# Keys before the query weights, one batch's cache rows per load, and transposed keys in the ring of load slots

## The chip, the core and the metric

The kernel runs on one core of a Trainium2 chip. The core has a matrix engine (PE, or TensorE), two engines for elementwise work (DVE, or VectorE, and ACT, or ScalarE), a general engine (POOL), and a queue engine (SP) that here issues the large loads; 16 DMA engines carry them out. On-chip memory (SBUF) has 128 partitions; a matrix product lands in a second, small memory (PSUM) of eight banks. The metric is the device time of one launch, in microseconds (us). A time of a profiled launch is its span, from the first to the last instruction, and a little around it.

## The reference

One decoding step for four sequences of one token: a pre-normed attention with a cache, and a gated feed-forward layer.

```python
W = 2048                                        # last 2048 cache rows
q = layernorm(x) @ wq                           # x 4 x 1024, wq 1024 x 4096: 32 heads of 128
k = k_cache[:, :, Sk - W:, :]                   # 4 batches x 4 groups x 2048 x 128; 8 heads share a group
v = v_cache[:, :, Sk - W:, :]
p = softmax(q . k * 128 ** -0.5)                # per batch and head, over 2048 rows
h = x + (p . v) @ wo                            # wo 4096 x 1024
g = layernorm(h)
out = h + (silu(g @ w1) * (g @ w3)) @ w2        # w1, w3 1024 x 3584, w2 3584 x 1024
```

Everything is bf16 in memory: wq, the keys, the values and wo are 8.4 MB each, w1, w3 and w2 7.3 MB each. Each is read once, 55.6 MB in all.

## The kernel before

**Loads.** All weights and cache rows go through a ring of ten slots of 16 KB per partition (`stream`, `NSLOT`). `jobs` lists 29 loads in the order wq (4), k (4), v (4), wo (4), w1 (4), w3 (4), w2 (5), of 2048 KB each (w1 and w3 1792 KB, the last two of w2 512 KB). SP issues them in this order (L114); load n waits until the last reader of load n-10 is done. A load of keys holds one group of all four batches, and each partition receives four runs of 16 cache rows, 4 KB each; a load of values holds one batch, again four runs of 4 KB per partition (one per group). A load of wo has two runs of 8 KB per partition; one of wq or w2 has 16 KB in one piece, and one of w1 or w3 14 KB.

**Queries.** x is normalized in transposed form (`layernorm_T`, L154 to L177). As each load of wq lands, PE multiplies (L202; four matmuls at a time use 32 columns of the array each). The queries are cast from PSUM by DVE and ACT (L211, L212), transposed on PE (L215), and put into a zero-padded operand `Qm` (L221), so that a batch and group meet only their own heads.

**Scores.** For each group, PE transposes the keys in blocks of 128 (256 transposes in all, L251), DVE and ACT copy them out of PSUM in turns (L257, L259), 8 blocks a copy, and PE multiplies `Qm` with them (L234) one step behind. The scores of all batches, groups and heads gather in one PSUM tile `sc_ps` of 128 x 2048 (four banks).

**Softmax and values.** Once for all: a row maximum on DVE (L268), one exponential on ACT with the row sums (L273), 16 transposes of the weights on PE (L283) and copies (L287, L289), 64 matmuls with the values (L296), a scaling with a mask that keeps each head's own group (L305), and four bf16 matmuls that regroup the rows (L315). Copies and a 32x32 block transpose on DVE (L319, L184, L324) give `oP`.

**The rest.** 128 matmuls with wo (L337), the residual and second layer norm (L346, then L154 to L177), 64 with w1 (L360), `eg` = silu of the gate on ACT and DVE (L372 to L375), 64 with w3 (L360 again), the product and a DVE transpose (L378, L184), 112 with w2 (L389), the residual (L399) and the store (L402).

The tile framework sets all waits and places the instructions of each engine in about the order written; each engine works through its own queue in order.

Of the kernel before, what the change touches and what calls it, by code (L numbers as in the profile page):

```python
# [10 lines left out]
P = 128  # L11
ACT = mybir.ActivationFunctionType
ALU = mybir.AluOpType
AX = mybir.AxisListType
BF16 = mybir.dt.bfloat16
FP32 = mybir.dt.float32

NSLOT = 10
SLOT = 8192


@with_exitstack
def kernel(
# [44 lines left out]
    T = 4  # L68
    GR = Hq // C
    wo_v = A_wo.rearrange("(k p t) n -> p k (t n)", k=GR, t=T)  # L70
# [6 lines left out]
    ktpool = ctx.enter_context(tc.tile_pool(name="ktpool", bufs=3))  # L77
# [4 lines left out]
    jobs = []  # L82
    for i in range(KC // 2):
        jobs.append(("wq", i, [2, NQ], wq_v[:, 2 * i : 2 * i + 2, :]))
    for g in range(Hkv):
        src = A_k_cache[:, g, Sk - W : Sk, :].rearrange("b (p j) d -> p b j d", j=NK)
        jobs.append(("k", g, [B, NK, Dh], src))
    for b in range(B):
        src = A_v_cache[b, :, Sk - W : Sk, :].rearrange("g (p j) d -> p g j d", j=NK)
        jobs.append(("v", b, [Hkv, NK, Dh], src))  # L90
    for i in range(GR // 2):
        jobs.append(("wo", i, [2, T * D], wo_v[:, 2 * i : 2 * i + 2, :]))
    for name, w_v in (("w1", w1_v), ("w3", w3_v)):
        for i in range(KC // 2):
            jobs.append((name, i, [2, F], w_v[:, 2 * i : 2 * i + 2, :]))
    W2B = [8, 8, 8, 2, 2]
    f0 = 0
    for i, n in enumerate(W2B):
        jobs.append(("w2", i, [n, D], w2_v[:, f0 : f0 + n, :]))
        f0 += n  # L100
    place = {(name, i): at for at, (name, i, _, _) in enumerate(jobs)}
    loaded = []

    def load_up_to(at):
        while len(loaded) < min(at, len(jobs)):
            name, i, shape, src = jobs[len(loaded)]
            slot = stream.tile([P, SLOT], BF16, tag="slot", name="s_" + name)
            n = int(np.prod(shape))
            view = slot[:, :n]
            if len(shape) == 2:  # L110
                view = view.rearrange("p (a b) -> p a b", a=shape[0])
            else:
                view = view.rearrange("p (a b c) -> p a b c", a=shape[0], b=shape[1])
            nc.sync.dma_start(out=view, in_=src)  # L114
            loaded.append(view)

    def get(name, i):
        at = place[(name, i)]
        load_up_to(at + NSLOT)
        return loaded[at]  # L120
# [4 lines left out]
    for c in range(C):  # L125
        nc.scalar.dma_start(out=x_nat[R * c : R * c + B, :], in_=x_flat[:, c * DQ : (c + 1) * DQ])
    load_up_to(NSLOT)
# [7 lines left out]
    gmask = const.tile([P, Hkv, 1], FP32)  # L135
    nc.vector.tensor_reduce(
        out=gmask[:, :, 0],
        in_=ident[:].rearrange("p (b g r) -> p g b r", b=B, g=Hkv),
        axis=AX.XY,
        op=ALU.add,  # L140
    )


    perm = const.tile([P, P], BF16)
    for b in range(B):
        nc.gpsimd.tensor_copy(
            out=perm[:].rearrange("p (l k b) -> p b l k", l=C, k=GR)[:, b],
            in_=ident[:].rearrange("p (b k l) -> p b l k", b=B, k=GR)[:, b],
        )
# [42 lines left out]

    q_ps = ps.tile([P, REP, Dh], FP32, tag="sc")
    HALF = REP // 2
    for i in range(KC // 2):
        w = get("wq", i)
        for kk in range(2):
            kc = 2 * i + kk
            for hf in range(2):
                for c in range(C):  # L200
# [8 lines left out]
                    )  # L209
    q_sb = act.tile([P, REP, Dh], BF16)  # L210
# [16 lines left out]
    sc_ps = ps.tile([P, W], FP32, tag="sc")  # L227
    JB = 4
    n_step = 0
    pending = []  # L230

    def emit_scores(g, nb, kT):
        for b in range(B):
            nc.tensor.matmul(  # L234
                sc_ps[R * b : R * b + R, nb * 512 : (nb + 1) * 512],
                lhsT=Qm[:, b, g * R : (g + 1) * R],
                rhs=kT[:, b],
                start=(g == 0),
                stop=(g == Hkv - 1),
                tile_position=(0, R * b),  # L240
            )

    for g in range(Hkv):
        k = get("k", g)
        for nb in range(NK // JB):
            kT = ktpool.tile([P, B, JB, P], BF16, tag="kT")
            for bb in range(2):
                kt_ps = ps.tile([P, 2, JB, P], BF16, tag=f"kt{n_step % 4}")
                for b2 in range(2):
                    for jj in range(JB):  # L250
                        nc.tensor.transpose(  # L251
                            out=kt_ps[:, b2, jj],
                            in_=k[:, 2 * bb + b2, nb * JB + jj, :],
                            identity=ident[:],
                        )
                if n_step % 2 == 0:
                    nc.vector.tensor_copy(out=kT[:, 2 * bb : 2 * bb + 2], in_=kt_ps[:])  # L257
                else:
                    nc.scalar.copy(out=kT[:, 2 * bb : 2 * bb + 2], in_=kt_ps[:])  # L259
                n_step += 1  # L260
            pending.append((g, nb, kT))
            if len(pending) > 1:
                emit_scores(*pending.pop(0))
    emit_scores(*pending.pop(0))


    rmax = act.tile([P, 1], FP32)
    nc.vector.reduce_max(out=rmax[:], in_=sc_ps[:], axis=AX.X)  # L268
    nmax = act.tile([P, 1], FP32)
# [163 lines left out]
```

## Time and profile before

| what | us |
|---|---|
| time, median of 3 runs (lowest, highest) | 140.75 (140.53, 141.15) |
| the profiled execution's own time | 140.66 |
| its span | 138.6 |
| PE busy | 68.6 |
| weight loads of PE busy | 41.1 |
| DVE busy | 33.0 |
| ACT busy | 26.2 |
| last load of wq landed (the matmuls that it releases start) | 22.83 |
| last load of v landed | 63.91 |
| weighted values scaled (L305 ends) | 69.80 |
| last load landed | 134.69 |

The profile names an instruction by line, engine, tile written and tiles read. Its chain that ended last goes back from the last instruction, at each step to what released it. A timeline gives the start, the duration, the instruction, how often it comes in a row, and in brackets how long its engine had been idle and what ended that. The granted clock (PEclk) is the TensorE clock that the throttle let through, in tenths of full speed. A DMA row in the chain runs from the issue of a load to its landing, so it includes the time that the load spends behind others.

### The profile page before, as it was taken

To read this page: it belongs to the slowest core of one execution; us is meant where nothing else is said; L and a number is where in the kernel's file an instruction comes from. 1 tells how busy PE (TensorE), PEld (TensorE's weight loads), DVE (VectorE), ACT (ScalarE), POOL (GpSimd) and SP (SyncE) were. 2 spreads that over 40 slices of the span, in tenths; PEclk is the share of its full clock that TensorE was granted. 3 is DMA by queue.
4 is the path that set the end of the run, shared out by engine and by line. 5 is a ranking of instruction groups with operands and counts; after the bars stand their busy time and mean duration, and the time that the engine had idled before them with its cause. 6 is when DMAs were issued, how large, how long until landed. Compare 5 with 4: busy or idle time off the path is not lost.

```text
span 138.6 us, 1940 instructions
## 1 busy us (share of the span) xinstructions
PE 68.6 (49%) x848; PEld 41.1 (30%) x848; DVE 33.0 (24%) x60; ACT 26.2 (19%) x27; POOL 3.3 (2%) x14
## 2 busy tenths in 40 slices
PE   0004634499898998029945225372240093352270
PEld 0002211197665674024333213220010041042150
DVE  0023000333443333701030003400019900610001
ACT  1100000125575756276000000400020000000000
POOL 8000000000000000000000000000000000000000
PEclk9999975557999999655896555555555559555559
DMA  5999999999999999999999999999999999999950
GB/s 147 437 407 444 435 421 398 410 411 415 422 420 418 420 420 418 421 425 434 425 430 421 425 438 438 423 430 434 430 430 434 426 434 444 421 421 444 389 207 2
DMA packets 7831, 55.70 MB, mean 402 GB/s; under 512 B 496, under 2 KB 528, under 8 KB 4880
## 3 DMA queue, kind: packets, MB, share of 16 engines
q1 hardware_dynamic: 7776, 55.58, 95.8%
q8 instruction: 6, 0.10, 0.2%
q10 hardware_dynamic: 48, 0.01, 0.0%
q14 instruction: 1, 0.01, 0.0%
HBM read 55.58 MB, written 0.01 MB: 401 GB/s over the span
## 4 chain that ended last, share of the span: by engine, by line
DMA 83%; PE 13%; DVE 1%; ACT 1%; issue 0%; ACTq 0%; SPq 0%
DMA s_w<-in_B_w_dram 47%; DMA s_v<-in_A_v_cache_dram 16%; DMA s_k<-in_A_k_cache_dram 14%; PE kt_ps L251 7%; DMA s_wq<-in_A_wq_dram 6%; PE o_ps L296 4%; PE sc_ps L234 2%; ACT kT L259 1%; DVE o_sb L305 0%; PE y_ps L389 0%; DVE res L399 0%; ACTq L259 0%; SPq L114 0%
## 5 line engine op out<-in xcount | busy, mean ns | idle before, releaser
L360 PE MATMUL gu_ps<-s_w,n_T 128*32 128x448 bf16 x128 | 12.3, 545 | 18.8 <-DVE eg L375 8.7
L251 PE MATMUL kt_ps<-ident,s_k 128*128 128x128 bf16 x256 | 18.4, 234 | 1.1 <-DMA s_k<-in_A_k_cache_dram 1.1
L259 ACT COPY kT<-kt_ps 128x1024 bf16<-128x1024 bf16 x16 | 15.9, 1013 | 13.0 <-PE kt_ps L251 13.0
L251 PEld LDWEIGHTS <-s_k 128*128 128x128 bf16 x256 | 16.3, 106 | 4.0 <-issue 2.7
L257 DVE COPY kT<-kt_ps 128x1024 bf16<-128x1024 bf16 x16 | 11.1, 692 | 15.8 <-PE kt_ps L251 15.8
L360 PEld LDWEIGHTS <-n_T 128*32 128x32 bf16 x128 | 4.9, 129 | 25.6 <-issue 20.1
L389 PE MATMUL y_ps<-s_w,hg_T 128*32 128x256 bf16 x112 | 6.7, 414 | 9.7 <-DMA s_w<-in_B_w_dram 9.6
L337 PE MATMUL y_ps<-s_wo,oP 128*32 128x256 bf16 x128 | 6.8, 381 | 8.5 <-DMA s_wo<-in_A_wo_dram 7.4
L202 PE MATMUL q_ps<-s_wq,n_T 128*32 128x512 bf16 x64 | 6.4, 557 | 7.6 <-DMA s_wq<-in_A_wq_dram 5.8
L234 PE MATMUL sc_ps<-kT,Qm 128*32 128x512 bf16 x64 | 9.1, 401 | 1.7 <-ACT kT L259 1.4
L389 PEld LDWEIGHTS <-hg_T 128*32 128x32 bf16 x112 | 4.7, 138 | 12.1 <-issue 7.0
L337 PEld LDWEIGHTS <-oP 128*32 128x32 bf16 x128 | 4.8, 128 | 10.1 <-issue 8.2
L157 PE MATMUL sums_ps<-both,ones_f 128*128 128x64 f32 x4 | 1.4, 447 | 11.7 <-DVE both L155 11.7
L167 ACT ACTIVATE rstd<-rstd,eps_t 128x4 f32<-128x4 f32 x2 | 0.6, 297 | 30.5 <-DVE rstd L166 30.5
L374 DVE RECIPROCAL eg<-eg 128x896 f32<-128x896 f32 x1 | 5.8, 5754 | 0.0
L296 PE MATMUL o_ps<-s_v,PT 128*32 128x512 bf16 x64 | 5.7, 497 | 0.1
L202 PEld LDWEIGHTS <-n_T 128*32 128x32 bf16 x64 | 2.3, 126 | 10.9 <-issue 10.6
L283 PE MATMUL pt_ps<-ident,Pm 128*128 128x128 bf16 x16 | 1.9, 312 | 6.0 <-ACT Pm L273 6.0
L157 PEld LDWEIGHTS sums_ps<-both,ones_f 128*128 128x128 f32 x4 | 1.0, 310 | 12.2 <-DVE both L155 12.2
L234 PEld LDWEIGHTS <-Qm 128*32 128x32 bf16 x64 | 2.3, 93 | 6.1 <-issue 4.9
L373 DVE TENSOR_SCALAR eg<-eg 128x896 f32<-128x896 f32 x1 | 0.6, 627 | 13.8 <-ACT eg L372 13.8
L346 DVE TENSOR_TENSOR h<-y_ps,x_nat 128x256 f32<-128x256 f32 x1 | 0.4, 425 | 14.3 <-PE y_ps L337 14.3
(54 smaller groups left out, 35.6 us busy)
## 6 DMA issues: line engine op xcount, KB each, us to landing
s_w<-in_B_w_dram SPq DMA_DIRECT2D x8, 1792.0 KB, 32.5
s_wq<-in_A_wq_dram SPq DMA_DIRECT2D x4, 2048.0 KB, 14.1
s_k<-in_A_k_cache_dram SPq DMA_DIRECT2D x4, 2048.0 KB, 19.4
s_v<-in_A_v_cache_dram SPq DMA_DIRECT2D x4, 2048.0 KB, 22.8
s_wo<-in_A_wo_dram SPq DMA_DIRECT2D x4, 2048.0 KB, 22.8
s_w<-in_B_w_dram SPq DMA_DIRECT2D x3, 2048.0 KB, 35.5
s_w<-in_B_w_dram SPq DMA_DIRECT2D x2, 512.0 KB, 31.3
x_nat<-in_A_x_dram ACTq DMA_DIRECT2D x4, 2.0 KB
```

Source lines behind the costliest of these rows:

```text
L157: nc.tensor.matmul(sums_ps[:], lhsT=ones_f[:], rhs=both[:], start=True, stop=True)
L202: nc.tensor.matmul(q_ps[R * c : R * c + R, hf * HALF : (hf + 1) * HALF, :], lhsT=xn_T[:, kc, :], rhs=w[:, kk, o : o + HALF * Dh], start=(k ...
L234: nc.tensor.matmul(sc_ps[R * b : R * b + R, nb * 512 : (nb + 1) * 512], lhsT=Qm[:, b, g * R : (g + 1) * R], rhs=kT[:, b], start=(g == 0), ...
L251: nc.tensor.transpose(out=kt_ps[:, b2, jj], in_=k[:, 2 * bb + b2, nb * JB + jj, :], identity=ident[:],)
L257: nc.vector.tensor_copy(out=kT[:, 2 * bb : 2 * bb + 2], in_=kt_ps[:])
L259: nc.scalar.copy(out=kT[:, 2 * bb : 2 * bb + 2], in_=kt_ps[:])
L283: nc.tensor.transpose(out=pt_ps[:, jj], in_=Pm[:, j * P : (j + 1) * P], identity=ident[:])
L296: nc.tensor.matmul(o_ps[R * b : R * b + R], lhsT=PT[:, j, R * b : R * b + R], rhs=vs[b][:, :, j, :], start=(j == 0), stop=(j == NK - 1), t ...
L337: nc.tensor.matmul(y_ps[R * c : R * c + R, :], lhsT=oP[:, k, t, :], rhs=w[:, kk, o : o + DQ], start=(k == 0 and t == 0), stop=(k == GR - 1 ...
L360: nc.tensor.matmul(out_ps[R * c : R * c + R, hf, :FH], lhsT=hn_T[:, kc, :], rhs=w[:, kk, o : o + FH], start=(kc == 0), stop=(kc == KC - 1) ...
L374: nc.vector.reciprocal(out=eg[:], in_=eg[:])
L389: nc.tensor.matmul(y2_ps[R * c : R * c + R, :], lhsT=hg_T[:, fc, :], rhs=w[:, ff, c * DQ : (c + 1) * DQ], start=(fc == 0), stop=(fc == FC ...
```

## The change

The kernel is rearranged up to the product with wo; what comes after is the same.

- **Order.** Four loads of keys come first, then wq, v, wo, w1, w3, w2. The keys are transposed before the queries are made.
- **Shape of the loads.** A load of keys, like one of values, now holds one batch, and partition i*4+g receives 64 neighbouring cache rows of group g, 16 KB in one piece. A load of wo has one piece of 16 KB per partition.
- **The ring.** Its list has 33 entries: k0 to k3, then kT0, wq0, kT1, wq1, kT2, wq2, kT3, wq3, then v, wo, w1, w3, w2. The four kT entries take a slot each for the transposed keys of one batch and load nothing, so seven loads are issued at first instead of ten. `done` marks an entry as used, and only then is the next one placed: wq3 takes the slot of k1, v0 that of k2, v1 that of k3, v2 that of kT0, v3 of wq0, wo0 of kT1, wo1 of wq1, wo2 of kT2, wo3 of wq2, w1's first of kT3.
- **Attention by batch.** Scores of one batch are 16 matmuls whose keys are read four elements apart; the partition of a score is its quarter and head. Then per batch: a row maximum on DVE, an fp32 matmul that turns it into a row, a maximum over the quarters, a copy, a one-row fp32 matmul that spreads it, an add of a mask; four exponentials on ACT (one per group, masked by the bias, written four elements apart); a DVE block transpose of 128 x 2048; an fp32 matmul for the sums; 16 matmuls over the full array with the values; a masked scaling and a sum over four on DVE. The batches are staggered by hand. The 16 PE transposes of the weights and their copies are gone.
- **Regrouping.** Eight fp32 matmuls (of 128 x 128 with 128 columns) with a sliding window of `strip` take the place of four bf16 ones.

```diff
+    ks = [("k", b, [JR, Dh], of_cache(A_k_cache, b)) for b in range(B)]
+    vs = [("v", b, [JR, Dh], of_cache(A_v_cache, b)) for b in range(B)]
+    kts = [("kT", b, [JR, P], None) for b in range(B)]
+    wqs = [("wq", i, [2, NQ], wq_v[:, 2 * i : 2 * i + 2, :]) for i in range(KC // 2)]
+    wos = [("wo", g, [1, T * D], wo_v[:, g : g + 1, :]) for g in range(Hkv)]
+    ring = ks + [x for two in zip(kts, wqs) for x in two] + vs + wos
...
+    def fill():
+
+        while len(views) < len(ring) and (len(views) < NSLOT or len(views) - NSLOT in used):
+            name, i, shape, src = ring[len(views)]
             slot = stream.tile([P, SLOT], BF16, tag="slot", name="s_" + name)
...
+    sc_ps = ps.tile([P, B, W // C], FP32, tag="sc")
...
+    def scores(b, gs):
+        v = get("kT", b).rearrange("p j (q i g) -> p g q j i", q=C, g=Hkv)
+        for g in gs:
+            for q in range(C):
+                nc.tensor.matmul(
+                    sc_ps[R * q : R * q + R, b, :],
+                    lhsT=Qm[:, b, g * R : (g + 1) * R],
+                    rhs=v[:, g, q],
...
+        if Hkv - 1 in gs:
+            done("kT", b)
+
+    def row_max(b):
+
+        rmax = act.tile([P, 1], FP32, tag="rmax", bufs=2)
+        nc.vector.reduce_max(out=rmax[:], in_=sc_ps[:, b], axis=AX.X)
+        mx_ps = ps.tile([P, P], FP32, tag="kt3")
+        nc.tensor.matmul(
+            mx_ps[:1, :], lhsT=rmax[:], rhs=ident_f[:], start=True, stop=True
+        )
...
+    def softmax(b):
+
+        nm_ps = ps.tile([P, Hkv], FP32, tag="kt3")
...
+        for g in range(Hkv):
+            nc.scalar.activation(
+                out=P4[:, :, :, g],
+                in_=sc_ps[:, b].rearrange("p (j i) -> p j i", i=L5),
+                func=ACT.Exp,
+                bias=bias[:, g : g + 1],
+                scale=qscale,
+                accum_out=rs[:, b, g : g + 1],
+            )
...
+    def transpose_p(b):
+        PT = ptpool.tile([P, JR, R], BF16, tag="PT")
+        nc.vector.transpose(
+            out=PT[:].rearrange("p j h -> p (j h)"),
+            in_=stage.pop(("P4", b))[:].rearrange("p j i g -> p (j i g)"),
+        )
...
+    def output(b):
...
+        for i in range(JR // JM):
+            nc.tensor.matmul(
+                o_ps[:],
+                lhsT=PT[:, i * JM : (i + 1) * JM, :].rearrange("p j h -> p (j h)"),
+                rhs=v[:, i * JM : (i + 1) * JM, :],
...
+        done("v", b)
...
+    for b in range(B + 1):
+        if b < B:
+            scores(b, (0, 1))
+        if b > 0:
+            row_max(b - 1)
+        if b < B:
+            scores(b, (2, 3))
+        if b > 0:
+            softmax(b - 1)
+        if b > 1:
+            transpose_p(b - 2)
+        if b > 2:
+            output(b - 3)
+    transpose_p(B - 1)
+    output(B - 2)
+    output(B - 1)
+    on_ps = ps.tile([P, 2, Dh], FP32, tag="kt2")
+    for l in range(2):
         for b in range(B):
             nc.tensor.matmul(
...
+                on_ps[:, l],
+                lhsT=strip[:, l, B - 1 - b : B - 1 - b + P],
+                rhs=om[:, b],
```

## The prediction

> **What bounds the kernel now.** I read the slices of the page first, then the chain in order of time, then stretches, then the timeline where the change cuts in.
>
> ```profile
> PEclk9999975557999999655896555555555559555559
> DMA  5999999999999999999999999999999999999950
> ```
>
> The DMA engines are full from the second slice nearly to the end; PE's granted clock is full only in places.
>
> ```profile
> 41.07 22.84 DMA s_v<-in_A_v_cache_dram
> ...
> 63.95 5.07 PE o_ps L296 x46
> ...
> 69.05 0.68 DVE o_sb L305
> 69.73 35.06 DMA s_w<-in_B_w_dram
> ...
> 104.86 29.84 DMA s_w<-in_B_w_dram
> ...
> 134.73 0.62 PE y_ps L389 x8
> ```
>
> The end is a load's landing at 134.69 and 0.62 of matmuls after it. Attention is done at 69.80 and everything behind it waits for weights: the loads set the pace, and attention has time to spare.
>
> ```profile
> 22.80:43.30 20.50, 17.74 (x197) 12.12 (x197) 6.73 (x14) 8.58 (x9) 0.00 (x0) 0.76 1.02 416
> 43.30:63.90 20.60, 13.74 (x170) 9.35 (x167) 8.82 (x12) 11.77 (x12) 0.00 (x0) 0.82 1.03 421
> 63.90:83.50 19.60, 10.29 (x161) 6.03 (x161) 1.55 (x4) 1.77 (x2) 0.00 (x0) 0.67 1.02 430
> 83.50:104.80 21.30, 9.32 (x98) 4.12 (x97) 4.05 (x13) 2.50 (x3) 0.00 (x0) 0.50 1.01 430
> ```
>
> The last two numbers are DMA share and GB/s: in runs of 4 KB (keys and values, the first two) full engines move 416 to 421, in longer runs 430.
>
> ```profile
> 22.83 1.90 PE L202 MATMUL q_ps<-s_wq,n_T 128*32 128x512 bf16 x16 [3.82 <-DMA s_wq<-in_A_wq_dram]
> 24.77 0.69 DVE L211 CAST q_sb<-q_ps 128x512 bf16<-128x512 f32 x1 [12.39 <-PE q_ps L202]
> 25.50 0.58 ACT L212 CAST q_sb<-q_ps 128x512 bf16<-128x512 f32 x1 [13.55 <-DVE q_sb L211]
> ...
> 59.34 1.97 ACT L273 ACTIVATE Pm<-sc_ps,nmax 128x2048 bf16<-128x2048 f32 x1
> ...
> 66.47 0.18 PEld L296 LDWEIGHTS <-PT 128*32 128x32 bf16 x4 [0.24 <-issue]
> 66.89 1.62 PEld L296 LDWEIGHTS <-PT 128*32 128x32 bf16 x29 [0.24 <-issue]
> ...
> 110.94 4.28 PE L360 MATMUL gu_ps<-s_w,n_T 128*32 128x448 bf16 x48 [8.66 <-DVE eg L375]
> ```
>
> Two things are to be seen. Pieces of one PSUM tile wait for each other: ACT's cast of the second half of q_ps waits for DVE's of the first, and w3's matmuls, into the other half of gu_ps, wait 8.66 for DVE to finish with w1's half. And PE's pace depends on its past: four side-by-side matmuls of 512 columns take 0.43 (0.18 and 0.24) until 66.89 and 0.22 after (29 weight loads in 1.62).
>
> **Against what the sum is made.** The profiled execution took 140.66: span 138.60, 2.06 around it; it lies 0.09 under the median of 140.75. No change means within 0.5% (139.95 to 141.35), about what a measurement of this kernel can tell.
>
> **The loads.** Eight loads of keys and values land from 22.83 to 63.91, 5.135 each. A wq load, in one piece of 16 KB per partition, took 4.86 (17.97 to 22.83). At that rate eight gain 2.2; by bytes moved (418 against 430) they gain 1.1, the lower bound. The four wo loads took 4.91; 0.2 more. So the last landing moves from 134.69 to 132.3 if the queue never runs dry.
>
> Three issues could let it. Seven loads are issued at first; wq3 then waits for the transposes of k1. k0 lands at 8.4 (as wq0 did), PE is free of the first layer norm at 10.8, and 64 transposes and eight copies take at most 5 per batch (two copies back to back on ACT take 1.93, so four take 4.05; 16 transposes 1.07): k1 is done near 20.6, k3 near 30, and the queue is full to 37. That work, on the path before, now lies under wq's loads. v2 is the tight one, since SP holds everything behind it until the scores of batch 0 free kT0. wq3 lands at 22.83 + 4 x 4.86 = 42.3; from landing to Qm it took 4.5 (22.83 to 27.34), so 46.8; 16 scores at 0.107 and a tail of 0.3: 48.8. v1 lands at 52.0. The only load into an empty queue took 7.64 from issue to landing: 56.4 for v2 against its turn at 56.9. Nothing lost, with 0.5 to spare. Later ones have more: kT1 is free at 51.6 and needed near 59, kT3 67.9 and 78, the first values 73.5 and 86, wo's first slot 103 and 103.5, close, but by then PE decides.
>
> **The attention chain, the part that decides.** Before, scores ran beside the keys' loads from 31 on, and from the last score (55.4) to the scaled values it took 14.4, all in engines' idle time. Now all scores wait for wq, at 48.8. If pieces of sc_ps wait for each other as those of gu_ps and q_ps do, the 16 score matmuls, the maximum and the exponentials of successive batches go one after another, in the order written. Per round: 8 score matmuls 0.9; maximum over 512 columns 0.65 (a quarter of 2.29 and a start); its fp32 matmul 0.7 to 1.1 (the layer norm's, with half the columns, took 0.69); 8 more score matmuls 0.5; the spreading matmul 0.7 (0.50 of fp32 weight loads come first); add 0.2; four exponentials at 0.66 (the 512-column cast on ACT is 0.585, reading the sum adds 0.08); hand-overs 0.5. That is 6.8 to 7.2. The first has 1.28 of table load: 57.0. The next two: 64.2 and 71.8 (DVE is transposing meanwhile). DVE's own queue delays the fourth: its maximum stands behind the block transpose of batch 1 (69.0 to 72.9) and the scaling and sum of batch 0 (PE ends that product at 73.5, then 0.75 and 0.6): it starts at 75.1, and the exponentials end at 81.0. A block transpose of 2048 columns is taken at 3.9, from 1.70 for 896. Then, in DVE's order: batch 2's transpose to 82.1, batch 1's product (PE done at 83.1) to 84.7, batch 3's transpose to 88.6, PE's 16 full-array matmuls to 92.1 (each streams 512 columns once, as a group of four side by side does: 0.22 warm), scaling and sum: 93.7, against 69.80 before.
>
> Behind it: eight fp32 matmuls at 0.74, 5.9 (each streams twice the layer norm's columns: 0.69 to 0.85 alone, less where weight loads overlap; nothing in the old four's 0.38 is like it), to 99.6; cast, transpose and copy 1.4, 101.0; 128 wo matmuls 5.7 (32 in 1.06 warm, 1.90 cold), 106.8; layer norm 4.1 (85.48 to 89.55), 110.8; w1, all landed, 4.9, 115.7; eg 8.7 (102.29 to 110.94), 124.4; w3 5.1, 129.6; product and transpose 3.1, 132.6; w2, landed but for its tail, 4.8, 137.4. Before, w2 ended at 135.35. **Sum: +2.05, so 142.7.** All the waits for weights (7.4 in wo, 8.4 in w1 and w3, 9.6 in w2) are eaten, and the saved 2.4 of loading is covered.
>
> **Prices that no row shows.** The score matmuls read keys four elements apart: taken as contiguous, since it is the nearest row; at twice the time the rounds grow by 3.3 and v2 lands 1.4 late. The Trainium skill (Advanced Engine Details and Errata, SBUF Cachelines) says two hits per 16-byte line are enough for full speed, which here they get; by it the price is nothing, as taken, and no run here shows it. Exponentials written four apart: 0.66, at most double, +7; nothing makes it cheaper than the cast. The DVE transpose reads contiguously here, in strides before: 2.2 (half a step per column) to 3.9, worth at most 1 off the chain, since PE and ACT hold the rounds. The additional constants of POOL and DVE, a dozen at 0.1 to 0.3, cost nothing: POOL is idle from 4 us, and DVE waits for x until 8.95; uncovered they would be 2 to 3.
>
> **Rivals.** *The loads still end last (faster).* If banks of sc_ps do not wait for each other, scores and maxima run ahead during exponentials, the fourth exponentials end near 76 and the chain is done at 88 instead of 93.7. It decides below 89.2, where w2 catches the last landing: 132.3 + 0.62 + 3.25 of store and rest + 2.06 = 138.2. Two waits on gu_ps and q_ps speak against it. DVE's queue being filled in another order could give half of it. 0.27 for any time under 139.95.
>
> *A draw.* The chain is 1.4 to 2.7 shorter than summed, by a shorter fp32 tail or transposes that fit in gaps: 140.7. 0.13.
>
> *A dearer chain.* Strided reads or writes or a cold clock: PE cold in all products adds 16 x 0.21 = 3.4 to the last one alone; 145 to 148. 0.09.
>
> *Long runs that collide.* A load of keys now takes pieces of four groups 2 MB apart in turn; if their reading got in each other's way, a load would take no less than 5.135. Loads of values have that distance in the trace of before, in 4 KB runs, without harm beyond 418 GB/s. Unchanged at 5.135, wq3 lands 1.1 later and the chain with it: 143.8; a like step above, 5.41, gives 144.9. 0.04. The Trainium skill (DMA: Bandwidth & Descriptors, Latency and other measured facts) has such a fall, 164 against 214 GB/s at a 2 MiB pitch of every partition; by that ratio an estimate is 6.3 per load and a time near 150; here only one partition in four steps that far, and the old values' loads do not show it.
>
> **How the numbers follow.** The sum holds with 0.47: 141.35 to 145, likeliest 142.7. With the draw 0.13, under it 0.27, dearer 0.09, collision 0.04: faster 0.27, same 0.13, slower 0.60. The range, 138.0 to 146.5, runs from the loads' bound, which nothing here undercuts by much, to half of the dearer case.
>
> **What would show it.** Right: keys and values 4.9 apart; no DMA gap near 52; PE at w1, w3 and w2 waiting for DVE, not for loads; regrouping finished after 92; the exponentials of a batch ending 7 after those of the one before; sc_ps matmuls released by ACT. Wrong: w2's matmuls released by DMA to the end (then 138), a DMA gap before v2 of over 2, or score matmuls over 0.2 apart.

## The result and the profile after

The changed kernel takes 146.43 us (median of four runs, 145.33 to 147.51) against 140.75 before: a ratio of 1.040, 95% interval 1.029 to 1.051. It is slower, as forecast, and by more than the likeliest 142.7; the time lies just inside the upper end of the range. The profiled execution took 145.38, with a span of 143.6. The four runs lie in two pairs, 145.3 and 147.5, and the slower pair had the higher mean granted clock (0.85 and 0.86 against 0.80); all readings below are of the profiled one.

Its chain in order of time (start, duration, what), from the last load of wq to the last matmuls:

```profile
8.69 24.01 DMA s_wq<-in_A_wq_dram
...
48.13 1.43 PE q_ps L241 x23
...
51.70 2.78 PE sc_ps L276 x20
...
57.04 4.95 ACT P L316 x8
62.01 2.32 DVE PT L328
...
68.07 4.96 ACT P L316 x8
...
79.60 4.97 ACT P L316 x8
...
104.24 1.05 DVE om L368
...
105.33 1.40 PE on_ps L391 x10
...
108.19 3.71 PE y_ps L416 x128
...
115.70 4.86 PE gu_ps L440 x62
...
122.19 5.76 DVE eg L455
...
129.19 4.93 PE gu_ps L440 x64
...
137.02 3.27 PE y_ps L470 x112
```

After 32.70 no load is on it. Before, 65 us of the chain behind attention were loads; now it is PE, DVE and ACT in turn from the first score at 51.70 to the end at 140.29, and the 112 matmuls of w2 run in one piece, because each of its loads has landed when its turn comes (the last at 138.98). The slices of the page say the same from the side of the loads:

```profile
PEclk9999855558999999555985568577799969955999
DMA  4999999999999999999999999999597999999910
```

The DMA engines are full to the 28th slice (100.5 us) and then run short for three (to 111.3): the second and third load of w3 wait for slots that PE holds, and land 5.99 and 7.00 behind the load before them, where 4.28 is usual. So the loads no longer set the end; they wait for it. In stretches (busy time and count of PE, weight loads, DVE, ACT, POOL; granted clock, DMA share, GB/s):

```profile
65.00:97.00 32.00, 24.09 (x93) 10.77 (x94) 14.06 (x25) 16.14 (x25) 0.00 (x0) 0.69 1.01 427
97.00:110.00 13.00, 8.51 (x95) 5.27 (x100) 5.25 (x9) 0.00 (x0) 0.00 (x0) 0.87 0.81 321
```

How the attention rounds go is seen in the timeline (start, duration, engine, line, instruction, and in brackets the idle time before it and what ended it):

```profile
27.84 1.90 PE L241 MATMUL q_ps<-s_wq,n_T 128*32 128x512 bf16 x16 [14.88 <-DMA s_wq<-in_A_wq_dram]
...
57.04 1.39 ACT L316 ACTIVATE P<-sc_ps,bias 128x512 bf16<-128x512 f32 x1 [4.84 <-DVE bias L313]
...
58.23 1.39 ACT L316 ACTIVATE P<-sc_ps,bias 128x512 bf16<-128x512 f32 x1
...
62.01 2.31 DVE L328 STREAM_TRANSPOSE PT<-P 128x2048 bf16<-128x2048 bf16 x1 [5.00 <-ACT P L316]
62.03 1.05 PE L276 MATMUL sc_ps<-s_kT,Qm 128*32 128x512 bf16 x8 [5.22 <-ACT P L316]
...
64.24 0.65 DVE L290 TENSOR_REDUCE rmax<-sc_ps 128x1 f32<-128x512 f32 x1
...
129.19 4.90 PE L440 MATMUL gu_ps<-s_w,n_T 128*32 128x448 bf16 x64 [8.67 <-DVE eg L456]
```

Four things are in it. PE stood idle for 14.88 with keys landed and untransposed, waiting for the first load of wq. An exponential is 1.39 to 1.41 long and starts 1.17 to 1.19 after the one before. The first half of batch 2's scores waits 5.22 until the last exponential of batch 0 has read the tile, though each batch has a bank of its own in it. And the next maximum, that of batch 1, stands in DVE's queue behind the block transpose (62.01 to 64.32). Its own scores were done at 56.49; what it waits for, by the tile, are those of batch 2, which are done at 63.08.

### The profile page after: what moved, and what is told of

It reads as the page before. It is cut to its first block, busy times and chain, and to the rows that moved or that the text cites. A ratio compares the mean times of both kernels' runs of the same rounds, so it can differ in the third digit from the quotient of the medians.

```text
span 143.6 us, 2032 instructions
## 1 busy us (share of the span) xinstructions
PE 79.2 (55%) x865; PEld 46.7 (32%) x868; DVE 52.0 (36%) x95; ACT 42.8 (30%) x56; POOL 4.1 (3%) x18
## 4 chain that ended last, share of the span: by engine, by line
PE 42%; DMA 22%; DVE 20%; ACT 12%; issue 2%; SPq 0%; DVEq 0%; ACTq 0%
DMA s_wq<-in_A_wq_dram 17%; ACT P L316 10%; PE o_ps L351 10%; PE kt_ps L223 9%; PE gu_ps L440 7%; DVE PT L328 6%; DMA s_k<-in_A_k_cache_dram 5%; PE sc_ps L276 4%; DVE eg L455 4%; PE q_ps L241 3%; PE y_ps L416 3%; PE y_ps L470 2%; PE nm_ps L305 1%; DVE hg_T L207 1%; DVE od L360 1%
## 5 line engine op out<-in xcount | busy, mean ns | idle before, releaser
L351 PE MATMUL o_ps<-s_v,PT 128*128 128x512 bf16 x61 | 23.3, 530 | 7.6 <-DVE PT L328 7.1
L316 ACT ACTIVATE P<-sc_ps,bias 128x512 bf16<-128x512 f32 x16 | 19.8, 1401 | 22.2 <-DVE bias L313 22.2
L227 ACT COPY s_kT<-kt_ps 128x1024 bf16<-128x1024 bf16 x16 | 15.8, 1012 | 21.8 <-PE kt_ps L223 21.8
L225 DVE COPY s_kT<-kt_ps 128x1024 bf16<-128x1024 bf16 x16 | 11.1, 691 | 25.2 <-PE kt_ps L223 25.2
L351 PEld LDWEIGHTS <-PT 128*128 128x128 bf16 x64 | 7.4, 129 | 19.8 <-DVE PT L328 9.3
L276 PE MATMUL sc_ps<-s_kT,Qm 128*32 128x512 bf16 x64 | 8.9, 607 | 7.9 <-ACT P L316 7.5
L328 DVE STREAM_TRANSPOSE PT<-P 128x2048 bf16<-128x2048 bf16 x4 | 9.2, 2306 | 10.0 <-ACT P L316 10.0
L470 PE MATMUL y_ps<-s_w,hg_T 128*32 128x256 bf16 x112 | 3.2, 273 | 2.9 <-DVE hg_T L207 2.9
L180 PEld LDWEIGHTS sums_ps<-both,ones_f 128*128 128x128 f32 x4 | 0.8, 249 | 11.6 <-DVE both L178 11.6
L416 PE MATMUL y_ps<-s_wo,oP 128*32 128x256 bf16 x128 | 3.7, 273 | 1.5 <-DVE oP L404 1.5
L316 ACT ACTIVATION_READ_ACCUMULATOR P<-sc_ps,bias 128x1 f32 x16 | 4.4, 276 | 0.0
```

The lines of the kernel that those rows point to most:

```text
L225: nc.vector.tensor_copy(out=kT[:, jb * JB : (jb + 1) * JB], in_=kt_ps[:])
L227: nc.scalar.copy(out=kT[:, jb * JB : (jb + 1) * JB], in_=kt_ps[:])
L276: nc.tensor.matmul(sc_ps[R * q : R * q + R, b, :], lhsT=Qm[:, b, g * R : (g + 1) * R], rhs=v[:, g, q], start=(g == 0), stop=(g == Hkv - 1) ...
L316: nc.scalar.activation(out=P4[:, :, :, g], in_=sc_ps[:, b].rearrange("p (j i) -> p j i", i=L5), func=ACT.Exp, bias=bias[:, g : g + 1], sca ...
L328: nc.vector.transpose(out=PT[:].rearrange("p j h -> p (j h)"), in_=stage.pop(("P4", b))[:].rearrange("p j i g -> p (j i g)"),)
L351: nc.tensor.matmul(o_ps[:], lhsT=PT[:, i * JM : (i + 1) * JM, :].rearrange("p j h -> p (j h)"), rhs=v[:, i * JM : (i + 1) * JM, :], start= ...
```

## The experiments

Theory: the loss is the attention chain, made long by four things, each of which can be taken away alone: the query matmuls that the framework put ahead of most key transposes, the dear exponentials, the whole-tile wait on `sc_ps`, and DVE's order. The rival says that the loads are slower in the new form, or that something behind attention grew. In all runs the kernel before runs on the same chip; ratios are to it, with 95% intervals. The floor that the loads set is 135.4 for the end of w2's matmuls (a time of 140.3 to 140.7); the changed kernel is 4.9 above it.

**Query matmuls behind all key transposes.**

```diff
-                nc.tensor.transpose(out=kt_ps[:, jj], in_=k[:, jb * JB + jj, :], identity=ident[:])
+                last_kt = nc.tensor.transpose(
+                    out=kt_ps[:, jj], in_=k[:, jb * JB + jj, :], identity=ident[:]
+                )
...
+                    with tc.issue_after(last_kt.ins):
                         nc.tensor.matmul(
                             q_ps[R * c : R * c + R, hf * HALF : (hf + 1) * HALF, :],
```

> The changed kernel, with the matmuls that make the queries pinned on PE behind the last transpose of the keys; nothing else. Theory: one such matmul stood in PE's queue after 24 of 256 transposes and waited 14.88 us for wq to land, so the scores began at 51.7 and not at the 46.8 that the arrival of wq's last load allows; expected: transposes done before 32, first scores at 47 (46.5 to 47.5), the whole chain 4.5 to 5 earlier, 140.5 to 141.2 us. Rival: the delay is made up later, because the rounds of the batches wait for something else (values, or DVE): then the exponentials of the last batch end where they did (94) and the time stays within 1 us of 145.4.

Measured: 141.49 (141.21 to 141.73), ratio 1.0057 (1.0039 to 1.0075). PE's timeline of this kernel:

```profile
10.68 19.37 PE L223 MATMUL kt_ps<-ident,s_k 128*128 128x128 bf16 x256
29.97 1.05 PE L244 MATMUL q_ps<-s_wq,n_T 128*32 128x512 bf16 x16
...
43.84 1.90 PE L244 MATMUL q_ps<-s_wq,n_T 128*32 128x512 bf16 x16 [2.99 <-DMA s_wq<-in_A_wq_dram]
...
48.11 2.33 PE L279 MATMUL sc_ps<-s_kT,Qm 128*32 128x512 bf16 x20 [0.35 <-DVE Qm L264]
```

All 256 transposes are done at 30.05 and the first scores start at 48.11 instead of 51.70. Both this start and the time lie a little above what was expected (46.5 to 47.5, and 140.5 to 141.2), because the last load of wq lands at 43.80, not at the 42.3 that was assumed. The profiled execution is 3.67 shorter (141.71 against 145.38): the start of the rounds is worth what it moved, one for one, though the exponentials still take 1.40 and the rounds still follow one another.

**Exponentials written in one run each**, and the block transpose reading them with strides instead.

```diff
-        P4 = ktpool.tile([P, JR, L5, Hkv], BF16, tag="P4")
+        P4 = ktpool.tile([P, Hkv, JR, L5], BF16, tag="P4")
...
-                out=P4[:, :, :, g],
+                out=P4[:, g],
...
-            in_=stage.pop(("P4", b))[:].rearrange("p j i g -> p (j i g)"),
+            in_=stage.pop(("P4", b))[:].rearrange("p g j i -> p j i g"),
```

> The changed kernel, with the exponentials written in one piece per group (the DVE block transpose then reads with a stride); nothing else. Theory: the 1.17 us per exponential (0.66 predicted) is the price of writing bf16 values 8 bytes apart; expected: 0.65 to 0.75 each, 2 us less per batch on ACT. The block transpose rises from 2.31 to 3.5 to 3.9 (1.90 ns per column in the strided rows of before). As DVE puts the transpose ahead of the next maximum, a part of the gain is lost there: rounds of 9.5 to 10.5 instead of 11.0, time 141 to 144 us. Rival: the exponential is dear for another reason (its bias, the read of the sums, PSUM while PE writes next to it): then it stays at 1.17 and the kernel gets slower by the dearer transposes, 146 to 149.

Measured: 144.77 (143.57 to 147.21 in four runs, the profiled one 144.02), ratio 1.0262 (1.0198 to 1.0327). The median lies above the 141 to 144 that was expected. ACT's and DVE's timelines:

```profile
56.76 0.69 ACT L316 ACTIVATE P<-sc_ps,bias 128x512 bf16<-128x512 f32 x1 [4.84 <-DVE bias L313]
...
57.44 0.68 ACT L316 ACTIVATE P<-sc_ps,bias 128x512 bf16<-128x512 f32 x1
...
59.58 3.73 DVE L328 STREAM_TRANSPOSE PT<-P 128x2048 bf16<-128x2048 bf16 x1 [2.85 <-ACT P L316]
63.24 0.65 DVE L290 TENSOR_REDUCE rmax<-sc_ps 128x1 f32<-128x512 f32 x1
```

The stride of the write is what makes the exponential dear: 0.69 and 0.67 apart in one run, 1.40 and 1.17 apart when written four elements apart. But the price moves to the transpose, 3.73 instead of 2.31, and the transpose stands ahead of the next maximum; the rounds shrink only from 11.0, 11.5 and 9.6 to 10.3, 9.5 and 9.4. Strides cost on either side.

**Scores in two PSUM tiles**, even batches in one and odd ones in the other (and the gate and up products with them, since they share the space).

```diff
-    sc_ps = ps.tile([P, B, W // C], FP32, tag="sc")
+    sc_two = [ps.tile([P, B // 2, W // C], FP32, tag=t, name="sc_ps" + t) for t in ("scA", "scB")]
...
-                    sc_ps[R * q : R * q + R, b, :],
+                    sc_two[b % 2][R * q : R * q + R, b // 2, :],
...
-    gu_ps = ps.tile([P, 4, 512], FP32, tag="sc")
-    up_projection("w1", gu_ps[:, 0:2])
+    g_ps = ps.tile([P, 2, 512], FP32, tag="scA")
+    u_ps = ps.tile([P, 2, 512], FP32, tag="scB")
+    up_projection("w1", g_ps)
```

> The changed kernel, with the scores in two PSUM tiles of two banks (even and odd batches), and gate and up products likewise in the two; nothing else. Theory: pieces of one PSUM tile wait for one another, and this alone makes a round of 11 us of scores, maximum and exponentials; expected: exponentials of successive batches 4.7 to 5.5 apart (ACT's own work), the last ending near 77 to 80 instead of 94, w3's matmuls no longer waiting for DVE; the chain then ends before the loads, which set the end at 138.0 to 139.0 us. Rival: the rounds are held by the order on PE and DVE, not by the tile: then they stay at 10 to 11, and only the 4.9 us of w3's matmuls are gained: 140 to 141.

Measured: 140.46 (140.2 to 140.55), ratio 0.9981 (0.9972 to 0.9991). The timeline:

```profile
55.46 0.67 DVE L290 TENSOR_REDUCE rmax<-sc_psscB 128x1 f32<-128x512 f32 x1
...
60.55 1.40 ACT L316 ACTIVATE P<-sc_psscA,bias 128x512 bf16<-128x512 f32 x1
...
61.72 1.49 ACT L316 ACTIVATE P<-sc_psscB,bias 128x512 bf16<-128x512 f32 x1
...
122.48 1.90 PE L471 MATMUL y_ps<-s_w,hg_T 128*32 128x256 bf16 x32 [3.21 <-DMA s_w<-in_B_w_dram]
127.37 1.90 PE L471 MATMUL y_ps<-s_w,hg_T 128*32 128x256 bf16 x32 [3.00 <-DMA s_w<-in_B_w_dram]
132.30 3.08 PE L471 MATMUL y_ps<-s_w,hg_T 128*32 128x256 bf16 x48 [3.03 <-DMA s_w<-in_B_w_dram]
```

The maximum of batch 1 now runs at 55.46, while batch 0's exponentials are still under way, so it needed nothing but its own scores. Batch 1's exponentials follow batch 0's without a gap, and batch 3's those of batch 2; batch 2, whose tile is batch 0's, still makes ACT wait 5.03. The fourth batch's end at 81.5 instead of 94.15, the values are done at 90.27 instead of 105.28, and w2 waits for its loads again. The wait between pieces of one PSUM tile was real, and without it the loss is gone. Two edits were made at once, but by an estimate the one to the scores would do: 90.27 and the 35.0 that the changed kernel needs behind its values give 125.3, well before the loads' 135.4. The time missed the 138.0 to 139.0 that was expected and lies in the rival's 140 to 141, without the rival's sign, rounds of 10 to 11. The rival on the loads' side falls too: the new load form is in this kernel and it is not slower.

**The up product alone in tiles of its own**, `sc_ps` as it was.

```diff
-    gu_ps = ps.tile([P, 4, 512], FP32, tag="sc")
-    up_projection("w1", gu_ps[:, 0:2])
+    g_ps = ps.tile([P, 2, 512], FP32, tag="sc")
+    up_projection("w1", [g_ps[:, 0], g_ps[:, 1]])
...
-    up_projection("w3", gu_ps[:, 2:4])
+    u0_ps = ps.tile([P, 512], FP32, tag="kt2")
+    u1_ps = ps.tile([P, 512], FP32, tag="kt3")
+    up_projection("w3", [u0_ps, u1_ps])
```

> The changed kernel, with the up products (w3) in two other PSUM tiles than the gate products; the scores stay in one tile. Theory: w3's 64 matmuls wait 8.67 us for DVE only because they share the tile; in another they run under the silu, and the product with the gate starts 4.9 us earlier: 140.2 to 141.0 us, unless the last loads of w2, which waited for slots around 100, are now the end (then up to 142.5). Rival: the wait is for something else of the silu: then w3's matmuls still start with its end and the time stays at 145.4.

Measured: 144.16 (142.07 to 145.71), ratio 1.0247 (1.0197 to 1.0298); the median misses the 140.2 to 141.0, and the 142.5 that was expected at most. PE's timeline of the profiled execution (142.07):

```profile
117.97 3.20 PE L440 MATMUL u_ps<-s_w,n_T 128*32 128x448 bf16 x64
129.81 3.61 PE L473 MATMUL y_ps<-s_w,hg_T 128*32 128x256 bf16 x64 [8.63 <-DVE hg_T L207]
...
136.46 0.40 PE L473 MATMUL y_ps<-s_w,hg_T 128*32 128x256 bf16 x8 [0.81 <-DMA s_w<-in_B_w_dram]
```

w3's matmuls lie under the silu, and from w1's first matmul (113.25) to w2's first it takes 16.6 instead of 21.3. The end gains less than these 4.8, because the late attention had already held back the slots: the last load lands at 136.42 here, against 134.7 where it is not held. And part of what the profiled execution shows is not of this edit: its values were done at 102.8 instead of 105.3, in code that is the same, because ten value matmuls in a row took 2.32 in it, at a granted clock of 1.00 (78.40 to 80.60), and 4.43 in the changed kernel's, at 0.50 (80.40 to 84.60). The times of this kernel spread over 3.6, so how much of the mean gain is the edit's is known only roughly.

**Only DVE's order**: the block transpose of a batch is placed behind the bias of the next.

```diff
-        nc.vector.tensor_tensor(out=bias[:], in0=nm_ps[:], in1=negm[:], op=ALU.add)
+        stage[("bi", b)] = nc.vector.tensor_tensor(
+            out=bias[:], in0=nm_ps[:], in1=negm[:], op=ALU.add
+        )
...
-        nc.vector.transpose(
+        with tc.issue_after(stage[("bi", min(b + 1, B - 1))].ins):
+          nc.vector.transpose(
```

> The changed kernel with the block transpose of a batch pinned on DVE behind the bias of the next batch; exponentials four apart as they were, one score tile. Theory: in the changed kernel the maximum waited 1.2 us per round behind the 2.31 us transpose, with the dear exponentials (4.95 a batch) the rounds become 9.2 to 9.9 instead of 11.0, and the time 141.5 to 144 us. Rival: the transposes come so late that the values' matmuls lose what the rounds gain: 145 or more.

Measured: 140.48 (140.04 to 141.39), ratio 1.000 (0.9976 to 1.0025): better than expected. DVE's and PE's timelines of the profiled execution (141.26):

```profile
62.96 0.69 DVE L290 TENSOR_REDUCE rmax<-sc_ps 128x1 f32<-128x512 f32 x1 [6.18 <-PE sc_ps L276]
...
65.78 2.30 DVE L331 STREAM_TRANSPOSE PT<-P 128x2048 bf16<-128x2048 bf16 x1
...
131.67 4.46 PE L473 MATMUL y_ps<-s_w,hg_T 128*32 128x256 bf16 x112 [2.93 <-DVE hg_T L207]
```

The maximum starts as soon as the matmuls that write the tile are done (batch 2's; its own scores had long been there), and the exponentials of batches 1 to 3 start at 65.89, 76.47 and 84.37 instead of 68.07, 79.60 and 89.19. With everything else dear as it was, w2 ends at 136.13, 0.7 above the loads' floor. The place of one instruction per batch in one queue was worth 4.1 (145.38 to 141.26).

**The same with the cheap exponentials**: the edits of the second and the fifth experiment together.

> The changed kernel with the exponentials in one piece and, on DVE, the block transpose of a batch pinned behind the bias of the next batch; one score tile, and the query matmuls where they were. Theory: with the exponential at 0.69 the rounds were still 10.3 and 9.5, because DVE, free while the exponentials ended, took the 3.7 us transpose first and the next maximum waited behind it (63.24 for scores ready at 60.6). Behind the bias it lies beside the exponentials: rounds of 6.8 to 7.6, as the prediction had them, last exponentials near 81 instead of 88.7, the chain under the loads: 140.3 to 141.2 us, against 144.0. Rival: PE holds the rounds, its value matmuls standing ahead of the maximum's: then rounds of 9 or more and 142.5 to 144.5.

Measured: 140.29 (140.03 to 140.54), ratio 0.997 (0.996 to 0.998). The first exponentials of the batches start at 56.61, 63.55, 73.66 and 81.06, the values are done at 95.66, and the last three groups of w2 wait for loads. The second round, 10.1, is outside the 6.8 to 7.6 that was expected (the others are 6.9 and 7.4), and in it the rival holds. DVE's and PE's timeline:

```profile
69.49 1.89 PE L354 MATMUL o_ps<-s_v,PT 128*128 128x512 bf16 x4
69.68 0.69 DVE L290 TENSOR_REDUCE rmax<-sc_ps 128x1 f32<-128x512 f32 x1 [2.62 <-PE sc_ps L276]
...
71.31 0.37 PE L292 MATMUL mx_ps<-ident_f,rmax 128*1 128x128 f32 x1
```

The maximum on DVE is done at 70.37, and the matmul that passes it on starts at 71.31, behind four value matmuls. All in all this is about the chain that the prediction drew (values done at 93.7), and its time is the loads' floor, not 142.7: the part behind attention is shorter than was summed.

**Order, exponentials and two tiles together** (the first three edits).

> The changed kernel with three mendings: query matmuls behind the key transposes, exponentials written in one piece, scores (and gate and up) in two PSUM tiles. Theory: with the two-tile version alone the last loads of w2 already landed when they did before (its w2 matmuls start at 122.48, 127.37 and 132.30, before 122.53, 127.32 and 132.30), so the loads are the end and a still shorter chain brings nothing: 140.2 to 140.6 us, with PE waiting for loads from w1 on. The weighted values are done before 80. Rival, the prediction's own bound: loads of 16 KB in one piece save 2.4, and the two-tile version was still held by something else: then 138.0 to 138.6.

Measured: 140.31 (140.18 to 140.59), ratio 0.9973 (0.9964 to 0.9981). No further gain over the two tiles alone: below the floor nothing is to be had from the chain. The values are done at 85.12, not before 80 as was expected, and it costs nothing. This and the one before are the best versions, 0.3% under the kernel before, less than the 0.5% that tells a change from none. Of the 2.2 which the prediction gave the loads some 0.4 are there, so the next three ask what the form of the loads is worth with this short chain.

**Keys and values in four loads of 512 KB**, first as 4 KB per partition, then one group at a time with 16 KB per partition.

```diff
-                nc.sync.dma_start(out=dst if name in ("k", "v") else view, in_=src)
+                if name in ("k", "v"):
+                    for c in range(4):
+                        nc.sync.dma_start(out=dst.rearrange("p (c x) -> c p x", c=4)[c], in_=src[c])
```

> The previous kernel with each load of keys and values issued as four of 512 KB, in which a partition receives 4 KB in one piece (another quarter of the cache rows each time, the same for keys and values, which changes no result). It is to be compared with the next kernel, which also issues four loads of 512 KB, but with 16 KB pieces. Theory now: 4 KB pieces take 4.98 per 2 MB (in the trace of before, past a step of one engine that every trace has once), 16 KB pieces 4.90: eight loads differ by 0.6, so 0.3 to 1.0 us over the next kernel. Rival, the prediction's term (5.135 against 4.86): 2.2 us over it.

```diff
+                        nc.sync.dma_start(out=dst.rearrange("(i g) x -> g i x", g=4)[c], in_=src[c])
```

> The kernel of the first run of this set with each load of keys and values issued as four of 512 KB, one per group, each with 16 KB pieces for 32 partitions. Theory: the pieces are as long as in one load, so the same 140.2 to 140.8 us as the first; if the four issues cost something (more loads in flight at once fill the queue's places), up to 1 more.

Measured: 143.16 (143.04 to 143.29), ratio 1.0173 (1.016 to 1.0187), and 141.29 (141.09 to 141.54), ratio 1.0043 (1.003 to 1.0055). Two prices come apart. Cutting a load in four costs 0.98 in all (141.29 against 140.31) at equal runs; 4 KB instead of 16 KB costs another 1.87, with landings 5.11 apart per 2 MB instead of 4.90. That is nearer to the rival's 2.2 than to the 0.3 to 1.0 that was expected.

**Keys and values in the form of before**, one load with four runs of 4 KB per partition.

```diff
-        return cache[b, :, Sk - W : Sk, :].rearrange("g (i j) d -> i g (j d)", j=JR)
+        return cache[b, :, Sk - W : Sk, :].rearrange("g (p j) d -> p g (j d)", j=JR // 4)
```

> The kernel with all three mendings, with the loads of keys and values in the very form of before: one load of 2048 KB, four runs of 4 KB per partition, one per group. Rows then lie at other partitions than the later steps take them from, so scores and values are mixed up; the amount of work of every engine is the same. Theory: past the one step that every trace has, 4 KB runs in this form took 4.97 per load and 16 KB runs 4.89, so the eight loads are 0.6 dearer and the time is 140.7 to 141.1 us, 0.4 to 0.8 over the same kernel with 16 KB runs (140.31). Rival, the prediction's term: 2.2 over it, 142.3 to 142.7 (four loads of 512 KB with 4 KB pieces instead of 16 KB ones cost 1.87).

Measured: 141.89 (141.81 to 142.08), ratio 1.0087 (1.0072 to 1.0102). The stretch from wq's last landing to the values' last, in the kernel of the three edits (columns as above):

```profile
43.80:63.40 19.60, 12.88 (x99) 4.68 (x99) 10.60 (x16) 7.33 (x18) 0.00 (x0) 0.59 1.00 425
```

The same stretch in the kernel with the old form:

```profile
44.30:64.90 20.60, 13.82 (x106) 4.86 (x106) 11.35 (x16) 7.33 (x18) 0.00 (x0) 0.70 1.04 415
```

Same bytes, 425 against 415 GB/s; landings of the values 4.89 apart against 5.15 on average (5.12 to 5.21). In this kernel the long runs are worth 1.58 (141.89 against 140.31), nearer to the rival's 2.2 than to the 0.6 that was expected. So the long runs do what the prediction said, and yet the kernel with them ends level with the one before. Where the difference goes is taken up below.

**The kernel before with w3's product in other PSUM tiles** (the edit of the fourth experiment, made to the kernel before).

> The kernel before, with the up products in other PSUM tiles than the gate products; nothing else. Theory: w3's matmuls no longer wait for the silu, but the loads are the end, so the time stays: 140.5 to 140.9 us, ratio within 0.3% of one. Rival: the wait for the silu delays slots and so loads: then 1 to 2 us are gained.

Measured: 140.68 (140.54 to 140.81), ratio 1.0003 (0.9993 to 1.0012). Its timeline:

```profile
105.01 1.68 PE L360 MATMUL u_ps<-s_w,n_T 128*32 128x448 bf16 x16 [2.55 <-DMA s_w<-in_B_w_dram]
...
117.74 1.68 PE L360 MATMUL u_ps<-s_w,n_T 128*32 128x448 bf16 x16 [2.57 <-DMA s_w<-in_B_w_dram]
```

The 8.66 that w3 waited for the silu are gone, the time is not: behind loads that end last, the longest wait of the page cost nothing. The same wait lies on the chain of the changed kernel.

**The kernel before with six slots** (`NSLOT = 6`).

> The kernel before with a ring of six slots in place of ten, nothing else; a load of w1 or w3 is then issued some 20 us before it lands, as in the changed kernels (16 to 20), where before has 33. Theory one, the short lead is what makes the same loads of w1 and w3 slower in the changed kernels (4.29 to 4.30 apart where before has 4.24 to 4.25): the eight land 4.29 apart here too, wo and w2 may grow alike, and the time is 141.1 to 141.6. Theory two, the lead has nothing to do with it: they stay at 4.24 to 4.25 and the time is 140.5 to 141.0. If the slots run dry while the values are multiplied, near 69, a landing gap of over 6 there adds its own excess over 4.9 to the time, and the spacing of the loads behind it still tells the two apart.

Measured: 140.69 (140.67 to 141.38), ratio 0.9999 (0.9984 to 1.0013). The eight loads of w1 and w3 take 34.02 from the last landing of wo to their own, 4.25 each, with 23.8 from issue to landing. So theory one falls: a shorter lead is not why they take 4.29 in the changed kernels.

## Why the prediction was right, and where it was not

**Right in sign and in mechanism.** The loss is where it was put: the loads stop setting the end, scores wait for wq, and the rounds go one after another because pieces of one PSUM tile wait for each other. Most signs that it named are there: w1, w3 and w2 wait for DVE and not for loads, there is no gap near 52, and regrouping ends at 106.7. One is not: the exponentials of a batch end 11.0, 11.5 and 9.6 after those of the one before, not 7. The waits from which it was read, on `gu_ps` and `q_ps` of before, carried over to `sc_ps`, and the two tiles took 5 us away. The time itself is partly luck: 146.43 is 0.07 inside the range, lies in the band of the rival with the dearer chain (145 to 148, chance 0.09) and not in that of the sum (141.35 to 145), and two large errors of opposite sign stand behind it.

**Strided reads.** The score matmuls cost what was taken, 0.43 for four (0.107 each), but that is not the price of contiguous reads. In the changed kernel both ran at a granted clock of 1.00, the query matmuls, which read in one piece, and the score matmuls, which read four elements apart (timeline, then stretches of `q_ps` and of `sc_ps` alone: busy time and count of PE, DVE, ACT; granted clock, DMA share, GB/s):

```profile
48.06 1.48 PE L241 MATMUL q_ps<-s_wq,n_T 128*32 128x512 bf16 x23
...
51.70 2.75 PE L276 MATMUL sc_ps<-s_kT,Qm 128*32 128x512 bf16 x24 [0.35 <-DVE Qm L261]
...
48.10:49.50 1.40, 1.40 (x23) 0.00 (x0) 0.00 (x0) 1.00 1.04 445
...
51.70:54.20 2.50, 2.50 (x24) 0.00 (x0) 0.00 (x0) 1.00 0.98 419
```

Groups of four contiguous ones start 0.22 apart, and 0.43 apart where the granted clock is 0.50 (27.84, sixteen in 1.90). Those of the scores start 0.43 apart at either clock (at 0.50 in the kernel with all three edits, sixteen in 1.91 from 48.09). The two kinds have the same shape and differ in the stride of what is read, though no run changes the stride alone. So the sum had the right number by luck: it took the contiguous price at half the clock. The Trainium skill (Advanced Engine Details and Errata, SBUF Cachelines) says that at least two hits on a 16-byte line are needed to absorb the latency; here each line gets two, and at full clock they are not enough. The Trainium skill's fall at a 2 MiB pitch (DMA: Bandwidth & Descriptors, Latency and other measured facts) does not show either: 4.89 per load.

**The step that failed first: "k1 is done near 20.6, k3 near 30".** The keys' transposes were to lie under wq's loads. The framework placed 16 query matmuls behind the first 24 transposes; the rest ran from 29.67 to 48.1, and `Qm` was ready and the first scores began at 51.70 instead of 46.8: +4.9. Of these 1.2 belong to the loads (wq3 landed at 43.54, by the trace's events, and not at 42.3; from there 4.5 gives 48.0) and 3.7 to the transposes, which is what the first experiment got back. The prediction assumed the order written and had no price for another. The slots went differently, too: all four loads of wq were issued by 10.06, wq3 into a free slot and not that of k1, to no effect.

**The rounds: "6.8 to 7.2".** The ends of the exponentials were forecast as 57.0, 64.2, 71.8 and 81.0 and came at 62.0, 73.0, 84.6 and 94.2. Of the 13.2, 4.9 are the late start, 3.8 and 3.9 the second and third round, and 0.4 the fourth. A round is longer by 2.3 of exponentials (4.95 against 2.65: the upper bound, "at most double", came true) and by 1.2 of the maximum behind the transpose (64.24 against 63.08); the rest is hand-overs. That order of DVE's queue is the second thing read from the code as written; with it mended, and nothing else, the loss is gone. A third thing was not in the sum either: the maximum of a batch waits for scores of a later batch in the same tile, which it does not read. In the first round the dear exponentials are hidden: the sum put 1.28 of table load on the path, and the trace has it at 50.92, beside the scores, so that from the scores' start to the exponentials' end it takes 10.3 against the 10.2 forecast, by luck. From the last exponential to the values it took 11.1 instead of 12.7, since a transpose takes 2.31 and not 3.9. The values are done at 105.28 instead of 93.7: +11.6.

**Behind attention: 35.0 instead of 43.7.** This is the error in the other direction, and why the total is near. Regrouping took 1.4 instead of 5.9: only five of its eight matmuls stand behind the last values (10 records in 1.38), and each takes 0.28, not 0.74. wo took 3.7 instead of 5.7 and w2 3.3 instead of 4.8: with all weights landed, PE runs them without a pause and is at its fast pace (128 in 3.68), where the sum took prices between fast and slow. The others were within 0.3 each. So +11.6 − 8.7 = +2.9: w2 ends at 140.29 instead of 137.4.

**The loads: "eight gain 2.2".** Loads of keys and values were forecast 4.86 apart and came 4.88 to 5.01 apart, nearly all 4.89 or 4.90; that is right, but the gain is not there. With the two tiles, w2's three large loads land at 122.44, 127.33 and 132.26; before, they landed at 122.43, 127.28 and 132.26. Three things ate it (landings by the semaphore events of the traces). First, the 5.135 per load of before was not the price of 4 KB runs: between two landings, 27.78 and 34.09, it has a single step of 6.31; without that, its loads are 4.97 apart on average (4.91 to 5.08). Second, every changed kernel has the like of that step once (24.00 after 18.09 with all three edits, 43.54 after 37.59 in the changed kernel itself), so nothing was saved by avoiding it. Third, loads that the change doesn't touch got slightly slower: wq 4.89 against 4.71 to 4.86, w1 and w3 mostly 4.29 against 4.24 to 4.25 (34.55 against 34.08 for these eight). The four loads of wo, to which the sum gave 0.2, take 19.59 against 19.61. The kernel with all three edits leads by 0.53 at the values' last landing (63.38 against 63.91), and by 0.08 at w3's. The lead of the issue is excluded as cause; what it is stays open. So does why the old form takes 5.15 in the changed kernel and 4.97 in its own.

**The rival on the other side.** It put the loads' bound at 138.2 and the deciding point at 89.2. Both were wrong, in opposite ways: the bound is 140.3, and a chain whose values are done at 95.66 still reaches it, because of the shorter part behind. Kernels that fit the rival's description come out the same as before, not faster by 2.

**Spread.** Kernels in which loads end last spread over 0.7 at most, usually under 0.5; the changed kernel over 2.2, and the ones with cheap exponentials alone and with the up product alone over 3.6. Value matmuls of 512 columns are 0.22 apart where the granted clock is 1.00 and 0.43 where it is 0.50, and the clock stood differently at the same place of two kernels; a chain adds that up and a load doesn't. Whether this makes the spread wasn't tried.

## What to carry to other kernels

Where loads set the end, a wait of 8.66 on the page costs nothing; what goes beyond the slack costs its full length. So before trading load time for a longer chain, compute where the chain ends, with the slow variants of each engine's price. Do not read the order of a queue from the source: two instructions placed otherwise than written (query matmuls ahead of transposes, a transpose ahead of a maximum) were worth 3.7 and 4.1, and pinning either took nearly all of the loss away. A PSUM tile shared by producers and consumers of different batches serializes them, even where each batch has a bank of its own: scores waited for exponentials of another batch, and a maximum for scores that it does not read. Two tiles of half the size undid that at no cost.

## What the runs showed that was not expected

- An exponential of 512 columns costs ACT 0.69 (0.67 apart) when its bf16 results are written in one run, and 1.40 (1.17 apart) when they are written four elements apart.
- A DVE block transpose of 128 x 2048 bf16 takes 2.31 reading in one run and 3.73 reading with strides; the results are the same size.
- Loads of 2 MB take 4.89 in runs of 16 KB and 5.11 to 5.15 on average in runs of 4 KB, in a kernel that is otherwise the same; in the kernel before, such runs took 4.97. The same bytes cut into four loads cost 0.98 more over eight of them.
- Score matmuls that read their keys four elements apart take 0.43 per group of four at a granted clock of 1.00 and of 0.50; matmuls of the same shape that read in one piece take 0.22 and 0.43.
- Each trace has one step of 0.6 to 1.7 beyond the usual distance between two landings, at 21 to 44 us, with its place moving between kernels. One of the 16 parts of a load comes late, the others in time (before: 15 by 32.97, the last at 34.09); its cause is open.
